# Two more k v products joined to other small products, the last gates in another order, and three moved steps in an attention and feed-forward kernel

## The chip, the cores and the metric

The kernel runs on one core of a Trainium2 chip. The time is the device time of one execution in microseconds (us); of several runs the median is given. The profile is of one further execution, whose own time is given beside it.

## The reference

```python
# q, k, v: (8, 8, 576, 64) = batch, head, sequence, head dimension
kv = np.einsum('bhsd,bhse->bhde', k, v)
out = np.einsum('bhsd,bhde->bhse', q, kv)
rms = np.sqrt(np.mean(out * out, axis=-1, keepdims=True) + 1e-06)
attn = out / rms * g_norm
# the bridge: heads side by side
x = attn.transpose(0, 2, 1, 3).reshape(4608, 512)
# the feed-forward part, d_ff = 1024
a = x @ w1
b = x @ w2
h = (a * b) @ w3
out = h @ w_out                        # (4608, 512)
```

Everything is float32. There is no softmax: attention is linear, so k v is a 64x64 matrix for each head.

## The kernel before

**What is worked on.** w3 and w_out are multiplied together once, early on (`fold_chunk`, L682, up to about 83 us), so that each token needs x, then `a * b` (the *gates*), then one product with the folded matrix (the *projection*). The 4608 tokens go in nine groups. Groups 0 to 7 hold 512 tokens of one batch each; the last 64 tokens of each of the eight batches, the *leftovers*, make up group 8. The loop `for n, T in enumerate(groups)` takes T in the order 0, 1, 2, 3, 4, 5, 6, 8, 7. While TensorE works on the gates of group T, the attention of batch T + 1 is strewn between its products.

**Strassen-Winograd products.** A gates stage multiplies 2x2 blocks with seven products in place of eight (`winograd`): sums of blocks s1 to s4 and t1 to t4 go in, and a11 b11, s1 t1, s2 t2, s4 b22, s3 t3, a12 b21, a22 t4 come out. The results are added up partly in the banks of PSUM (a product may be accumulated on top of an older one in the same bank) and partly by VectorE; c11, c12, c21, c22 are the four blocks of the result. Each product is four matmuls of 128x256 (L708), so a stage has 28. In the profile a matmul counts as two instructions, the weight load and the product: "x56" is one stage. ScalarE copies a bank that is still needed to SBUF (`keep`, L726: p1, p5, u2, u3), VectorE forms the c and multiplies its a half by its b half. Where `done` gets two summands it adds them on VectorE first; with one (c21) ScalarE copies one half (L854), and VectorE multiplies the other by it.

**Stages.** Of the four quarters of d_ff, p0 to p3, groups 0 and 1 do each in a gates stage of its own. Groups 2 to 8 (`IN_TWO`) do, in this order: gates p2; p0 and p1 together in a two-level Winograd product (`gates_of_two`, 98 matmuls of 128x128, L976, in two halves w = 0, 1 with seven products n each); gates p3, the *last gates*; and `project_twice` (L1223, again two-level, 98 matmuls). Between these stand `sum_ab` and `sum_ab_two`, which form the sums that the projection takes in, and `sum_inner`, which forms the inner sums of one of its seven products (numbers 0 to 6; `sum_inner(1, 2)` does two at once in instructions of twice the size). In the last gates VectorE's order is written by hand: `following` says what comes after which c. The inner sums of 1 and 2 are formed after c21, that is, after the last product.

**Attention pieces.** `steps(b)` lists what batch b does, in eight places fs[0] to fs[7]; one is run at each call of `between()` in group b - 1. In groups 2 to 6, places 0 and 1 lie in gates p2, 2 to 5 after products 2 and 5 of the two halves of `gates_of_two`, and 6 and 7 in the last gates. The pieces: `kv(g)`, k v of four heads, 36 small matmuls (L335), six copies to SBUF on ScalarE (L343, L345); `product(h)`, q times k v of four heads (L413) and the norm behind it (square, reduce, root, multiply); `product_left`, the same for the leftovers of two batches, for odd b only (L432). `kv(0)` of batch b + 1 is run in fs[6] while batch b is the current one, that is, in the last gates; `begin_kv` then issues the loads of `kv(1)`, and where g is 1 the loads of the next batch's k and v. These small products take their banks from `ps_at` (3 banks, the gates have `ps_mm`, 5 banks); the first bank of `product` comes from `ps_mm` if `of_mm` says so.

**Turns.** q and x must be transposed. Their pieces are `turn`, `begin` and `end`: copies on ScalarE, a DMA transpose, copies back. For b of 2 and over `turns_by_scalar` hangs each one on a *slot*: a name of a place such as ("p1", "u2"), run by `run_slot` right after the copy u2 of stage p1 has been issued. For b = 1 `steps` does it with `begin` and `end` behind a copy given by name. `end` of a q turn also issues the load of the next batch's q (`load_q_ahead`).

**Order and queues.** The order of TensorE, GpSimd and SyncE is that of the program. ScalarE and VectorE are ordered by a scheduler, with hints (`issue_after`), except VectorE in the last gates and the projection. SyncE's DMA queue issues in order: q, k, v, the streamed blocks of the weights (`load_w`), and those of the folded matrix (`load_b`, some of which go out on ScalarE's queue), and the stores.

Of the kernel before, what the change touches and what calls it, by code (L numbers as in the profile page):

```python
# [22 lines left out]
def kernel(  # L23
# [32 lines left out]
    nc = tc.nc  # L56
# [261 lines left out]
    def attention(b):  # L318
# [4 lines left out]
        def start():  # L323
            xT[b] = work.tile([P, 2, 2, NP // 2, N], FP32, name="xT")

        def kv(g):

            k_sb, v_sb = (loaded[name, b, g] for name in "kv")
            kv_ps = [bank(ps_at, "at")[:, 0:D] for _ in range(2)]
            for j in range(JS):  # L330
                cols = slice(j * D, (j + 1) * D)
                for r in range(2):
                    for e, ps in enumerate(kv_ps):
                        rows = slice(e * HP, (e + 1) * HP)
                        nc.tensor.matmul(  # L335
                            ps[r * D:(r + 1) * D, :],
                            lhsT=k_sb[rows, r, cols],
                            rhs=v_sb[rows, r, cols],
                            start=(j == 0),
                            stop=(j == JS - 1),  # L340
                        )
            for e, ps in enumerate(kv_ps):
                nc.scalar.copy(kv_b[:, 0, e, g, :], ps)  # L343
                for r in range(2):
                    copies["kv"] = nc.scalar.copy(  # L345
                        kv_b[(1 - r) * D:(2 - r) * D, 1, e, g, :], ps[r * D:(r + 1) * D, :]
                    )
# [51 lines left out]
        def product(h):  # L399

            of_mm = b and not (h and b > FIRST_OF_TWO)
            o_ps = [bank(*((ps_mm, "mm") if of_mm else (ps_at, "at"))), bank(ps_at, "at")]
            for m in range(4):
                r, e = 2 * h + m // 2, m % 2
                for i in range(2):
                    n = 2 * m + i
                    for t in range(2):
                        tokens = slice(t * L, (t + 1) * L)  # L410
                        for l in range(2):
                            rows = slice(l * D, (l + 1) * D)
                            nc.tensor.matmul(  # L413
                                o_ps[l][tokens, n * D:(n + 1) * D],
                                lhsT=qT[r][rows, e, i, tokens],
                                rhs=kv_b[rows, m // 2 ^ l, e, h, :],
                                start=True,
                                stop=True,
                            )
            xn = st[h] = work.tile([P, 2, 2, 4, D], FP32, name="xn", bufs=1)  # L420
            return norm(o_ps, [xn[:, :, l].rearrange("p i m d -> p m i d") for l in range(2)])

        def product_left():

            xn = st["left"] = work.tile([P, NP, 2, D], FP32, name="xn_left", bufs=1)

            o_ps = [bank(ps_at, "at") for _ in range(2)]
            for r in range(NP):
                for l in range(2):
                    for e in range(2):  # L430
                        rows = slice(e * D, (e + 1) * D)
                        nc.tensor.matmul(  # L432
                            o_ps[e][l * L:(l + 1) * L, r * D:(r + 1) * D],
                            lhsT=st["qT"][rows, r, l * L:(l + 1) * L],
                            rhs=kv_sb[(b - 1 + l) % 3][rows, r % 2 ^ e, e, r // 2, :],
                            start=True,
                            stop=True,
                        )
            o_ps = [t[:, 0:NP * D] for t in o_ps]
            all_of(norm(o_ps, [xn[:, :, e:e + 1, :] for e in range(2)]))  # L440

# [35 lines left out]
            elif b + 1 < B:  # L477
                load_q(b + 1, r + 2 - NP)

        def begin_kv(g):  # L480
            kv(g)
            if g == 0:
                load_four("kv", b, 1)
            elif b + 1 < B:
                load_four("kv", b + 1, 0)
# [38 lines left out]
    def turns_by_scalar(b):  # L524
# [14 lines left out]

        def end(name):  # L540
            all_of(turning[name])
            if name[0] == "q" and name[1] != "left":
                batch(name[1]).load_q_ahead(name[2])

        if b > FIRST_OF_TWO:
            q_begins, q_ends = ((0, 0), (0, 0)), ((0, 6), (1, 0))
# [20 lines left out]
        if b + 1 < B:  # L567
            n = batch(b + 1)
            for r in range(2):
                at(("p3", "u2"), begin, ("q", b + 1, r), n.q_by_dma, r)  # L570
                at(("proj", "u2"), end, ("q", b + 1, r))

    def steps(b):

# [26 lines left out]
        if b == 1:  # L601
# [8 lines left out]
                    all_of(t)  # L610

            ends[1].append((end_first,))
        fs[2 if b == 1 else 1] += [(a.begin_kv, 1), (a.finish, 0)]
        if b == 1:
            last = {}

            def begin(name, behind, f, *args):
                last[name] = f(*args)
                with tc.issue_after(copies[behind][-1].ins):
                    next(last[name])  # L620
                next(last[name])

            def end(name, behind):
                with tc.issue_after(copies[behind][-1].ins):
                    next(last[name], None)
                all_of(last[name])

            fs[2] += [(begin, f"q{r}", "u2", a.q_two_by_dma, r) for r in (2, 3)]
            fs[3].append((begin, "left", "u3", a.q_left_by_dma))
            fs[4].append((begin, "x", "u3", a.x_by_dma, 0, nc.scalar.copy))  # L630
            ends[4] += [(end, "q2", "p1"), (end, "q3", "p5")]
            ends[5] += [(end, "x", "u2"), (end, "left", "u3")]
        elif by_scalar:
            turns_by_scalar(b)
        else:
            turn(1, a.q_two_by_dma, 2, 3)
            turn(2, a.x_by_dma, 0)
            if odd:
                turn(1, a.q_left_by_dma)
        second = 5 if b == 1 else 4  # L640
        if more:
            fs[6 if in_two else second].append((batch(b + 1).begin_kv, 0))
        fs[second].append((a.finish, 1))
        if odd:
            fs[3 if in_two else second + 1].append((a.product_left,))
# [51 lines left out]

    def winograd(
        lhsT, rhs, chunks, done, between=lambda: None, keep_u3=True, after=lambda: None,
        places=(2, 1, 0),  # L700
    ):


        def product(a_name, b_name, to=None):
            ps = to if to is not None else bank(ps_mm, "mm").rearrange("p (u n) -> p u n", u=2)
            for u in range(2):
                for c in range(chunks):
                    nc.tensor.matmul(  # L708
                        ps[:, u, :],
                        lhsT=lhsT(a_name, u, c),  # L710
                        rhs=rhs(b_name, c),

                        start=(u == 0 and c == 0 and to is None),
                        stop=(c == chunks - 1),
                        skip_group_check=True,
                    )
            after()
            return ps

        def keep(name, ps):  # L720
            if name == "p1":
                t = pair_of_sums[:, 0].rearrange("p s c t -> p (s c) t")
            else:
                t = late_slots(places[("p5", "u2", "u3").index(name)])
# [2 lines left out]
            run_slot((stage[0], name), copies[name][-1])  # L727
            late[name] = t
            return t

        r1 = product("a11", "b11")
        p1 = keep("p1", r1)
# [111 lines left out]
    def gates(T, p, between, ready=lambda name: None):  # L844
# [4 lines left out]
        def multiply(name, one, two):  # L849
# [14 lines left out]
            lambda name, c: xb[T][name][:, c, :],  # L864
            NP // 2, done, between, T == 0 or p + 1 < NF,
            places=(2, 1, 0) if T not in IN_TWO else (0, 1, 2) if p + 1 == NF else (2, 0, 1),
        )


# [287 lines left out]

    inner = {}

    def sum_inner(*ns, between=lambda: None):  # L1160

        x_1 = ab[1].rearrange("p f j n -> p j f n")
        if ns == (1, 2):
# [2 lines left out]
            x = x_1  # L1166
        else:
            n, = ns
            x = {0: ab[0][:, :, 0], 3: ab_sums[2], 4: ab[0][:, :, 1], 6: x_1[:, 1]}[n].unsqueeze(1)
        a11, a12, a21, a22 = (  # L1170
            x[:, :, 2 * j:2 * j + 2, i * P:(i + 1) * P] for i in range(2) for j in range(2)
        )
# [2 lines left out]
        else:  # L1175
            s1, s2, s4 = (
                t.unsqueeze(1) for t in (
                    inner_sums[n % 4 // 3] if n < 6 else [pair_of_sums[:, 0, i] for i in range(3)]
                )
            )  # L1180
        nc.vector.tensor_add(s1, a21, a22)
        nc.vector.tensor_sub(s2, s1, a11)
        nc.vector.tensor_sub(s4, a12, s2)
        between()
        nc.vector.tensor_sub(a21, a11, a21)
        for i, n in enumerate(ns):
            inner[n] = [t[:, i] for t in (a11, a12, a22, s1, s2, s4, a21)]

    def project_twice(T, last, ahead, load_after):
        def store(half):  # L1190
# [99 lines left out]
        products(3, r2)  # L1290
        if not done[T]:
            load_b()
        if last:
            sum_inner(6)
            finish(p1, 0, 0)
# [140 lines left out]
    for n, T in enumerate(groups):  # L1436
# [44 lines left out]
        for p in range(NF):  # L1481
# [2 lines left out]
            stage[0] = f"p{p}" if T in IN_TWO or T == FIRST_OF_TWO - 1 else None  # L1484
            if T and p + 1 == NF:
                sum_1, sum_2, sum_4, sum_3 = sum_ab(p)
                following = {
                    "c12": [], "c22": [sum_1], "c11": [lambda: sum_inner(0, between=sum_2)],
                    "c21": [*of_two, lambda: sum_inner(1, 2), sum_3, sum_4],
                }  # L1490
# [100 lines left out]
```

## Time and profile before

| what | before |
|---|---|
| three runs | 746.58, 746.49, 746.93 us |
| median | 746.58 us |
| the profiled execution | 747.45 us |
| its span in the trace | 745.7 us |
| its granted TensorE clock | 1.0 |

The span is from the first to the last recorded instruction. By stretches of the span, busy microseconds of each engine and the share of the time in which the core's DMA engines are busy:

| stretch (us) | what runs | PE | VectorE | ScalarE | DMA |
|---|---|---|---|---|---|
| 0 to 83 | w3 times w_out, batch 0 | 79.41 | 68.11 | 60.55 | 0.93 |
| 131 to 217.4 | gates of group 1 and what lies ahead | 85.53 | 65.47 | 37.05 | 0.90 |
| 217.4 to 239.74 | projection of group 1 | 22.13 | 20.56 | 8.20 | 0.94 |
| 239.74 to 313.54 | group 2 | 73.80 | 63.80 | 40.63 | 0.85 |
| 313.54 to 386.52 | group 3 | 72.98 | 63.24 | 38.05 | 0.82 |
| 533.30 to 606.03 | group 6 | 72.73 | 63.67 | 35.48 | 0.65 |
| 606.03 to 673.97 | group 8 (leftovers) | 67.94 | 58.06 | 17.50 | 0.53 |

Groups 4 and 5 are like 2 and 3 (73.80 and 72.98 long). Where PE's time equals the length of the stretch, TensorE had no gap that the trace shows. An instruction's line is that of the function that issues it; the lines of helpers (L708, L726, L1025) are shared by all their callers, so a stage is told by its place in time or its tile.

### The profile page before, as it was taken

The page shows a single profiled execution, that of the slowest core. Times are in us where ns is not written, and L with a number is a line of the kernel's source. Part 1 is how long each engine was busy: PE and PEld are TensorE (multiplying, and loading weights), DVE is VectorE, ACT ScalarE, POOL GpSimd, SP SyncE. Part 2 cuts the span into 40 slices and gives each one's busy share as a digit, 9 for nine tenths or more (in the row PEclk, how much of TensorE's full clock was granted, in tenths as well). Part 3 has the DMA queues.
Part 4 walks back from the last instruction along what each step waited for, and adds up shares of the span by engine and source line. Part 5 has one row for each costly group of instructions (what it writes and reads, how often), then busy time and mean ns, then how long its engine had stood idle before and what let it go on. Part 6 is the DMA issues. An engine that isn't in the chain of part 4 may idle for free.

```text
span 745.7 us, 16769 instructions
## 1 busy us (share of the span) xinstructions
PE 737.3 (99%) x6843; PEld 658.5 (88%) x6843; DVE 632.7 (85%) x1212; ACT 371.2 (50%) x638; POOL 21.5 (3%) x29
## 2 busy tenths in 40 slices
PE   8999999999999999999999999999999999999998
PEld 5455788888899999999999999999999999999997
DVE  6987998967868699979996999799969987997797
ACT  6687878414552575256526752575267313212321
POOL 0000000131000000010000000000001000000000
PEclk9999999999999999999999999999999999999999
DMA  9996934598999689968987898579847672465454
GB/s 310 365 308 215 263 107 122 124 333 288 275 310 329 172 218 268 312 165 233 276 284 169 252 295 270 179 240 265 290 107 218 209 224 87 157 228 166 133 199 136
DMA packets 135456, 169.65 MB, mean 228 GB/s; under 512 B 78036, under 2 KB 110804, under 8 KB 135380
## 3 DMA queue, kind: packets, MB, share of 16 engines
q1 hardware_dynamic: 132928, 154.16, 68.9%
q10 hardware_dynamic: 2452, 14.42, 5.6%
q8 instruction: 54, 0.88, 0.5%
q14 instruction: 22, 0.18, 0.1%
HBM read 130.55 MB, written 20.71 MB: 203 GB/s over the span
## 4 chain that ended last, share of the span: by engine, by line
PE 94%; DMA 2%; DVE 1%; ACT 1%; issue 0%; SPq 0%; ACTq 0%; DVEq 0%
PE mm L708 38%; PE mm L1223 22%; PE mm L976 21%; PE mm L682 7%; PE at L335 2%; PE at L413 1%; DMA raw<-in_moe_w_out_dram 1%; PE at L669 1%; DMA w3o_sb<-w3o_l 1%; PE mm L413 1%; DMA raw<-in_moe_w_dram 0%; PE at L1266 0%; PE at L432 0%; ACT w_sb L133 0%; DVE c L859 0%; ACT qT L296 0%
## 5 line engine op out<-in xcount | busy, mean ns | idle before, releaser
L1025 ACT COPY slots<-mm 128x512 f32<-128x512 f32 x88 | 51.6, 586 | 131.4 <-PE mm L1223 73.4
L708 PE MATMUL mm<-xT,w_sb 128*128 128x256 f32 x480 | 110.2, 379 | 0.0
L708 PEld LDWEIGHTS mm<-xT,w_sb 128*128 128x128 f32 x480 | 90.4, 190 | 12.1 <-issue 0.5
L708 PE MATMUL mm<-xc,ws 128*128 128x256 f32 x352 | 79.8, 380 | 0.9 <-ACT inner_sums L726 0.9
L708 PEld LDWEIGHTS mm<-xc,ws 128*128 128x128 f32 x352 | 66.9, 190 | 10.2 <-ACT inner_sums L726 1.3
L726 ACT COPY slots<-mm 128x512 f32<-128x512 f32 x61 | 35.8, 587 | 70.9 <-PE mm L708 66.7
L682 PE MATMUL mm<-chunks,ab 128*128 128x512 f32 x128 | 60.7, 605 | 1.2 <-DVE chunks L172 1.2
L1029 DVE TENSOR_TENSOR slots<-mm,slots 128x512 f32<-128x512 f32 x66 | 45.3, 686 | 17.7 <-PE mm L976 17.3
L1026 ACT COPY slots<-mm 128x384 f32<-128x384 f32 x88 | 42.4, 482 | 24.9 <-PE mm L1223 22.3
L976 PE MATMUL mm<-ws,w3o_sb 128*128 128x128 f32 x350 | 54.0, 275 | 0.0
L1223 PE MATMUL mm<-w3o_sb,ab 128*128 128x128 f32 x368 | 48.7, 275 | 0.2 <-DMA w3o_sb<-w3o_l 0.2
L976 PEld LDWEIGHTS mm<-ws,w3o_sb 128*128 128x128 f32 x350 | 46.4, 192 | 0.0
L1223 PEld LDWEIGHTS mm<-w3o_sb,ab 128*128 128x128 f32 x368 | 45.4, 192 | 0.8 <-issue 0.4
L381 DVE TENSOR_REDUCE inv<-sq 128x8 f32<-128x512 f32 (+1 forms) x40 | 24.5, 628 | 25.3 <-ACT sq L380 25.0
L1223 PE MATMUL mm<-w3o_sb,raw 128*128 128x128 f32 x340 | 43.5, 275 | 0.0
L708 PE MATMUL mm<-xc,w_sb 128*128 128x256 f32 x176 | 42.4, 384 | 0.3 <-ACT slots L726 0.3
L682 PEld LDWEIGHTS mm<-chunks,ab 128*128 128x128 f32 x128 | 21.6, 190 | 22.9 <-issue 14.3
L1223 PEld LDWEIGHTS mm<-w3o_sb,raw 128*128 128x128 f32 x340 | 40.7, 192 | 0.0
L708 PE MATMUL mm<-xT,ws 128*128 128x256 f32 x160 | 38.5, 384 | 0.0
L708 PEld LDWEIGHTS mm<-xc,w_sb 128*128 128x128 f32 x176 | 32.8, 190 | 5.3 <-ACT slots L726 0.7
L1030 DVE TENSOR_TENSOR slots<-mm,slots 128x384 f32<-128x384 f32 x66 | 36.4, 551 | 0.9 <-PE mm L1223 0.9
L854 ACT COPY c<-mm 128x256 f32<-128x256 f32 x22 | 8.2, 371 | 54.1 <-PE mm L708 51.2
(230 smaller groups left out, 1634.2 us busy)
## 6 DMA issues: line engine op xcount, KB each, us to landing
w3o_sb<-w_l SPq DMA_DIRECT2D x21, 896.0 KB, 5.3
w3o_sb<-w3o_l SPq DMA_DIRECT2D x18, 896.0 KB, 4.7
raw<-in_moe_w_dram SPq DMA_DIRECT2D x31, 512.0 KB, 7.8
raw<-w3o_l SPq DMA_DIRECT2D x15, 896.0 KB, 4.8
w3o_sb<-w3o_l ACTq DMA_DIRECT2D x14, 896.0 KB, 4.7
k_sb<-in_k_dram SPq DMA_DIRECT2D x16, 576.0 KB, 4.9
v_sb<-in_v_dram SPq DMA_DIRECT2D x16, 576.0 KB, 6.1
q_sb<-in_q_dram SPq DMA_DIRECT2D x32, 256.0 KB, 4.5
```

The costliest lines, as they stand in the source:

```text
L335: nc.tensor.matmul(ps[r * D:(r + 1) * D, :], lhsT=k_sb[rows, r, cols], rhs=v_sb[rows, r, cols], start=(j == 0), stop=(j == JS - 1),)
L381: adds["norm"] = nc.vector.tensor_reduce(out=inv[:, i], in_=sq.rearrange("p (h d) -> p h d", d=D), axis=AX.X, op=ALU.add)
L413: nc.tensor.matmul(o_ps[l][tokens, n * D:(n + 1) * D], lhsT=qT[r][rows, e, i, tokens], rhs=kv_b[rows, m // 2 ^ l, e, h, :], start=True, st ...
L682: nc.tensor.matmul(sums_ps[half][m], lhsT=w3T[half, c][:, m, :], rhs=chunks[:, c, 1, :], start=(c == 0), stop=(c == KF - 1),)
L708: nc.tensor.matmul(ps[:, u, :], lhsT=lhsT(a_name, u, c), rhs=rhs(b_name, c),  start=(u == 0 and c == 0 and to is None), stop=(c == chunks ...
L726: copies.setdefault(name, []).append(nc.scalar.copy(t, ps))
L976: nc.tensor.matmul(ps[place // 4][:, place % 4, :], lhsT=x, rhs=y, start=new and place // 4 not in seen, stop=True, skip_group_check=True,)
L1025: nc.scalar.copy(z[:, 0:4], ps[0])
L1026: return nc.scalar.copy(z[:, 4:7], ps[1][:, 0:3])
L1029: nc.vector.tensor_add(z[:, 0:4], ps[0], z[:, 0:4])
L1030: nc.vector.tensor_add(z[:, 4:7], ps[1][:, 0:3], z[:, 4:7])
L1223: nc.tensor.matmul(ps[place // 4][:, place % 4, :], lhsT=x[:, c, :], rhs=y[:, c, :], start=new and place // 4 not in seen, stop=(c == 1), ...
```

## The change

- `kv` and `begin_kv` take `beside`, banks to put k v in: the last D columns of each. `kv(0)` of the next batch leaves the last gates of groups 2 to 5. For odd b over 2 `product_left` calls it with its own two banks, after its matmuls; for even b it goes in place `second` (4) ahead of `finish(1)`, which runs `product(1)`. For even b the first bank of that product comes from `ps_mm` now.
- The last gates of groups 2 to 8 go another way through `winograd` (`copy_first`). The order of the products becomes a11 b11, s1 t1, s2 t2, a12 b21, s3 t3, s4 b22, a22 t4. ScalarE copies a11 b11 from its bank into a second bank, r3, and a12 b21 is accumulated on top of it, so c11 comes out of one bank like c21 did. u3 is copied to the tile `inner_sums` (where p1 was kept). In groups 3 and 5 the first bank comes from `ps_at`.
- VectorE's order in these last gates: `following` has one sum each of inner 0, 1 and 2 in chosen places (`steps_of_inner` returns them one at a time), and 1 and 2 are no longer done as a pair.
- Group 1, gates: the remaining steps of the norm of batch 2's first q k v product (`begin_first`) go in the slot behind p1 of stage p1. Group 0: the turn of q3 begins one place later, behind u3. Projections: the load of q for the batch after (`load_q_ahead`) goes from the end of the q turn into the slot ("proj", "loads"), after `products(3)` and its `load_b`.

```diff
-        def kv(g):
+        def kv(g, beside=None):
...
-            kv_ps = [bank(ps_at, "at")[:, 0:D] for _ in range(2)]
+            kv_ps = [t[:, -D:] for t in beside or [bank(ps_at, "at") for _ in range(2)]]
...
-            of_mm = b and not (h and b > FIRST_OF_TWO)
+            of_mm = b and (h == 0 or b <= FIRST_OF_TWO or b % 2 == 0)
...
+            if FIRST_OF_TWO < b < B - 1:
+                batch(b + 1).begin_kv(0, o_ps)
             o_ps = [t[:, 0:NP * D] for t in o_ps]
...
         def end(name):
             all_of(turning[name])
-            if name[0] == "q" and name[1] != "left":
-                batch(name[1]).load_q_ahead(name[2])
+            if name[0] == "q" and name[1] == b:
+                a.load_q_ahead(name[2])
...
                 at(("proj", "u2"), end, ("q", b + 1, r))
+                at(("proj", "loads"), n.load_q_ahead, r)
...
-        fs[2 if b == 1 else 1] += [(a.begin_kv, 1), (a.finish, 0)]
+        def begin_first():
+            rest = a.product(0)
+            next(rest)
+            slots.setdefault(("p1", "p1"), []).insert(0, (all_of, rest))
+
+        fs[2 if b == 1 else 1] += [
+            (a.begin_kv, 1), (begin_first,) if by_scalar and not in_two else (a.finish, 0),
+        ]
...
-            fs[2] += [(begin, f"q{r}", "u2", a.q_two_by_dma, r) for r in (2, 3)]
+            fs[2].append((begin, "q2", "u2", a.q_two_by_dma, 2))
+            fs[3].append((begin, "q3", "u3", a.q_two_by_dma, 3))
...
         if more:
-            fs[6 if in_two else second].append((batch(b + 1).begin_kv, 0))
+            if not (in_two and odd):
+                fs[second].append((batch(b + 1).begin_kv, 0))
...
         def keep(name, ps):
-            if name == "p1":
+            if name == "p1" or copy_first and name == "u3":
...
+        if copy_first:
+            r1 = halves(first if first is not None else bank(ps_mm, "mm"))
+            r3 = halves(bank(ps_mm, "mm"))
+            product("a11", "b11", r1, new=True)
+            copies["p1"].append(nc.scalar.copy(r3, r1))
+            run_slot((stage[0], "p1"), copies["p1"][-1])
+            r2 = product("s1", "t1")
+            p5 = keep("p5", r2)
+            product("s2", "t2", r1)
+            u2 = keep("u2", r1)
+            between()
+            product("a12", "b21", r3)
+            done("c11", r3, None)
+            product("s3", "t3", r1)
+            done("c22", p5, keep("u3", r1))
+            product("s4", "b22", r2)
+            between()
+            done("c12", r2, u2)
+            product("a22", "t4", r1)
+            done("c21", r1, None)
+            return
...
+            copy_first=T in IN_TWO and p + 1 == NF,
+            first=bank(ps_at, "at") if T in IN_TWO and p + 1 == NF and T % 2 and T + 2 < B else None,
...
+        return [
+            lambda: nc.vector.tensor_add(s1, a21, a22),
+            lambda: nc.vector.tensor_sub(s2, s1, a11),
+            lambda: nc.vector.tensor_sub(s4, a12, s2),
+            lambda: nc.vector.tensor_sub(a21, a11, a21),
+        ]
...
+        for f, *args in slots.pop(("proj", "loads"), []):
+            f(*args)
...
+                zero, one, two = (steps_of_inner(n) for n in range(3)) if T in IN_TWO else [None] * 3
                 following = {
+                    "c11": zero[0:3], "c22": [],
+                    "c12": [sum_1, sum_3, sum_2, one[0], zero[3], one[1]],
+                    "c21": [
+                        one[2], one[3], *of_two, two[0], sum_4, two[1], two[2], two[3],
+                    ],
+                } if T in IN_TWO else {
                     "c12": [], "c22": [sum_1], "c11": [lambda: sum_inner(0, between=sum_2)],
                     "c21": [*of_two, lambda: sum_inner(1, 2), sum_3, sum_4],
                 }
```

More of the change, by code (lines that the diff above doesn't have):

```diff
@@ L478, in load_q_ahead, with begin_kv @@
                 load_q(b + 1, r + 2 - NP)
-        def begin_kv(g):
-            kv(g)
+        def begin_kv(g, beside=None):
+            kv(g, beside)
             if g == 0:
@@ L699, in winograd, with halves, product @@
         lhsT, rhs, chunks, done, between=lambda: None, keep_u3=True, after=lambda: None,
-        places=(2, 1, 0),
+        places=(2, 1, 0), copy_first=False, first=None,
     ):
-        def product(a_name, b_name, to=None):
-            ps = to if to is not None else bank(ps_mm, "mm").rearrange("p (u n) -> p u n", u=2)
+        def halves(ps):
+            return ps.rearrange("p (u n) -> p u n", u=2)
+        def product(a_name, b_name, to=None, new=False):
+            new = new or to is None
+            ps = halves(bank(ps_mm, "mm")) if to is None else to
             for u in range(2):
@@ L711, in product @@
                         rhs=rhs(b_name, c),
-                        start=(u == 0 and c == 0 and to is None),
+                        start=(u == 0 and c == 0 and new),
                         stop=(c == chunks - 1),
@@ L1158, with steps_of_inner @@
     inner = {}
-    def sum_inner(*ns, between=lambda: None):
+    def steps_of_inner(*ns):
         x_1 = ab[1].rearrange("p f j n -> p j f n")
@@ L1168, in sum_inner @@
             n, = ns
-            x = {0: ab[0][:, :, 0], 3: ab_sums[2], 4: ab[0][:, :, 1], 6: x_1[:, 1]}[n].unsqueeze(1)
+            x = {
+                0: ab[0][:, :, 0], 1: ab_sums[0], 2: ab_sums[1], 3: ab_sums[2], 4: ab[0][:, :, 1],
+                6: x_1[:, 1],
+            }[n].unsqueeze(1)
         a11, a12, a21, a22 = (
@@ L1177, in sum_inner @@
                 t.unsqueeze(1) for t in (
-                    inner_sums[n % 4 // 3] if n < 6 else [pair_of_sums[:, 0, i] for i in range(3)]
-                )
-            )
[L1181 to L1185, printed above, removed]
+                    [pair_of_sums[:, n % 2, i] for i in range(3)] if n in (1, 2, 6)
+                    else inner_sums[n % 4 // 3]
+                )
+            )
         for i, n in enumerate(ns):
             inner[n] = [t[:, i] for t in (a11, a12, a22, s1, s2, s4, a21)]
+        return [
[4 more added lines that the diff above has]
+        ]
+    def sum_inner(*ns, between=lambda: None):
+        *others, replace = steps_of_inner(*ns)
+        all_of(f() for f in others)
+        between()
+        replace()
     def project_twice(T, last, ahead, load_after):
```

## The prediction

> **What bounds the kernel now.** I read the page's first part, then who waited for whom, then the chain of waits, then the timelines of single stages.
>
> ```profile
> span 745.7 us, 16769 instructions
> ...
> PE 737.3 (99%) x6843; PEld 658.5 (88%) x6843; DVE 632.7 (85%) x1212; ACT 371.2 (50%) x638; POOL 21.5 (3%) x29
> ```
>
> TensorE is never free for long, and the chain of waits lies on it for 94% of the span, at a granted clock of 1.0. So a change can pay in two ways only: fewer microseconds of TensorE work, or fewer gaps in it. After 83 us the waits of PE are three:
>
> ```profile
> PE mm L708 <- ACT inner_sums L726: 0.9, 1, 0.9
> PE mm L708 <- ACT slots L726: 0.3, 1, 0.3
> PE mm L1223 <- DMA w3o_sb<-w3o_l: 0.2, 1, 0.2
> ```
>
> The chain (start, length, what) gives the price of each block, because a block of equal length that is interrupted or not can be compared:
>
> ```profile
> 313.54 10.36 PE mm L708 x48
> 323.90 1.21 PE at L335 x72
> ...
> 326.05 1.93 PE mm L708 x8
> 327.97 15.63 PE mm L976 x140
> 343.60 1.09 PE at L413 x64
> 344.69 6.45 PE mm L976 x56
> 351.14 5.18 PE mm L708 x24
> 356.32 1.21 PE at L335 x72
> 357.53 7.10 PE mm L708 x32
> ...
> 571.72 12.09 PE mm L708 x56
> 583.80 22.22 PE mm L1223 x196
> 606.03 12.09 PE mm L708 x56
> 618.12 21.88 PE mm L976 x196
> ```
>
> A gates stage alone is 12.09, 196 instructions of 128x128 alone are 21.88. From these: k v and q kv together cost 327.97 - 313.54 - 12.09 = 2.34; q kv alone costs 351.14 - 327.97 - 21.88 = 1.29; k v alone costs 364.63 - 351.14 - 12.09 = 1.40. Apart they are 2.69, so a place where the two follow each other saves 0.35. In the same way leftovers alone (group 2, 254.17 to 278.16, less 21.88 and 1.29) cost 0.82. Groups 2 to 5 hold nothing beyond these blocks: 73.80 = 67.94 + 2.34 + 0.82 + 1.29 + 1.40 within 0.01. The gaps are elsewhere: 0.34 in group 6's projection (22.22 for 21.88), 0.45 in group 1's (217.41 to 239.74), 1.13 in group 1's gates (173.61 to 196.08 is 22.47; 88 L708 instructions and 2.34 make 21.34), and about 0.4 at 121.4 in group 0.
>
> **The joined k v.** In groups 2 to 5 the 36 matmuls leave the last gates: for odd b (groups 2, 4) they go behind the leftovers, for even b (3, 5) ahead of the second q kv product. Four joins at 0.35 are 1.40. Those with q kv repeat a pair that the trace shows. One with the leftovers isn't shown; it saves between 0 and 0.35, and I take 0.35, as both are 64x64 blocks like the shown pair. So 1.40, at least 0.70.
>
> What moves with them: six ScalarE copies (L343, L345) and two loads of 576 KB on SP. At 174.87 the six take 1.32. In groups 3 and 5 they end about when the q kv product does, and the two squares behind them start 0.3 late; ScalarE has 0.48 of waiting next (345.82), so nothing is passed on. In groups 2 and 4 they stand ahead of the leftovers' squares and of the copy of the next p1 (L1025, 267.68 to 268.27), which TensorE needs at 268.89: cover 0.62. k v gives the queue 1.05 more on PE; 1.32 of copies and a square of 0.28 then push that copy to about 269.86, against 269.94 for PE. I take 0.1 lost over both groups, from 0 to 0.4.
>
> Here the Trainium skill speaks against the join: "TensorEngine Tiling (Array Packing)", Performance Considerations, PSUM Bottleneck, says that tiling speeds up TensorE but not the emptying of PSUM, which may become the bottleneck. Were the emptying the bound, 1.32 - 0.62 = 0.70 would be lost in each of two groups, 1.40 in all, and the sum would be 1.2 instead of 2.6. The row's 4.3 us of ScalarE idle in the same group's last gates (before 291.69) says the queue is late in places only, so I stay with the rows.
>
> The two loads move before SP's q loads in groups 2 and 4, behind them in 3 and 5. DMA is busy 0.91 of 264 to 278 and 0.95 of the last gates, so 1.15 MB (some 5 us at 216 GB/s) displace what follows by about 5. q at 267.92 took 4.4 and is copied at 284.17; the three w3o loads from 274.84 on are needed from 291.7 on. Both have more than 5 left. The k v loaded for the leftovers' place is issued at 251.3 and 251.84 and lands in 5.7 and 6.7, by 258.5, needed at 263.9.
>
> **The last gates (groups 2 to 8).** TensorE's 28 matmuls stay 28. ScalarE gets r3<-r1, u3 and one c21 copy, and loses p1: +0.58 + 0.37 per group, on an engine that is half idle. VectorE loses the 0.69 add of c11, and sums of inner 1 and 2 become eight of 0.42 for four of 0.69: +0.6; net 0. What counts is when each must be ready, counted from the start of the last gates (s), with VectorE free at 8.1 as before (L1071 ends 8.17 after 278.16):
> - r3 copy: starts 1.77, PE overwrites r1 at 3.45. Bank to bank isn't shown; the nearest rows are 0.37 (128x256) and 1.18 (L158, 128x1024). Cover 1.68 holds both. I take 0.58, the row of equal size.
> - c11: PE done 6.91; ScalarE has two qT copies to 7.9, c21 to 8.3, the multiply to 8.7, three sums to 9.9; the projection (12.09) needs them from 13.4 on.
> - c22 waits for u3 (9.3), is done by 11.0; c12 by 12.2; then sum_1, sum_3, sum_2, one, zero's last: 13.97, needed 14.77. Cover 0.8, the thinnest. c21's multiply ends 14.6.
> - inner 1: s4 and s3 by 15.4, needed 17.45 and 17.9. Before, s3 came at 18.78 after its start and was needed at 19.3 with k v's 1.4 in between; in group 6, without k v, that was the 0.34 of 22.22.
> So nothing is lost, and the 0.34 goes. If VectorE were 1 later, every group would lose 0.2.
>
> **Group 1's gates.** ScalarE's queue (start, length):
>
> ```profile
> 177.71 0.37 ACT L854 COPY c<-mm 128x256 f32<-128x256 f32 x1 [0.43 <-PE mm L708]
> 181.17 0.31 ACT L385 ACTIVATE inv<-inv,eps_col 128x16 f32<-128x16 f32 x1 [3.09 <-DVE inv L381]
> 181.38 0.56 ACT L726 COPY inner_sums<-mm 128x512 f32<-128x512 f32 x1
> 181.85 1.04 ACT L296 COPY qT<-q_sb 128x1024 uint16<-128x1024 uint16 x1
> 182.80 0.58 ACT L726 COPY slots<-mm 128x512 f32<-128x512 f32 x1
> ```
>
> The root waits 3.09 for VectorE, and p1's copy stands behind it. After, p1 goes at 179.2 and PE goes on at 180.97. But VectorE's reduces still end at 181.13 (its backlog comes from a DMA at 173.76), the root and one qT copy still come before p5, so p5 ends at 182.91 and PE wants it at 182.7: a gap of 0.25 and the restart of 0.11 (2.00 for 1.89). The two xn products move behind seven sums to 185.83, xT's two copies behind them to 187.8, u3 to 188.38, PE wants it at 188.24: 0.15 and 0.11 again. So 1.13 becomes 0.65, gain 0.48; from 0.2 to 1.13.
>
> **Group 1's projection.** The load for its last product is issued at 229.95, behind two q loads (228.40), and takes 6.3; the median of the tile's loads is 4.7. With the q loads behind it lands at 234.7, before 236.2. Gain 0.45, from 0. In other groups SP's order is unchanged.
>
> **Group 0.** The second qT copy (1.05) and its transpose move behind u3. But the root before u3 waits for reduces that end at 120.97, and it started at 121.00. Gain 0.03, from 0 to 0.4; the qT copies then end 1 us later, with 2.8 of ScalarE idle at 132.55.
>
> **Sum.** 1.40 - 0.10 + 0.34 + 0.48 + 0.45 + 0.03 = 2.6. The profiled execution has a span of 745.7 and took 747.45; so 743.1 and 744.85. The runs' median is 746.58, 0.87 below the profiled one; the same 2.6 off gives 744.0.
>
> **Rivals.**
> - All gaps go: 1.40 + 0.34 + 1.13 + 0.45 + 0.40 = 3.72, so 742.9. For: each edit sits at a gap. Against: VectorE's backlog at 181.13 and 120.97 isn't touched. 0.10.
> - Only the joins pay; the gaps reappear where p5, u3 or another queue is next: 745.2. For: VectorE is 85% busy and 21.09 of 21.9 in group 2's projection. Against: sums that come 2 earlier. 0.14.
> - The change doesn't do what it says: the joins save nothing, because k v's 1.40 is work wherever it stands; 2.6 - 1.4 leaves 745.4. Against: the pair at 323.90. 0.05.
> - Slower: in groups 2 and 4 q lands late behind k v. ScalarE's qT copies then hold c11's c21 copy and VectorE behind it. I expect landing near 280.5 and use at 285.2, and 0.8 of cover in the projection. It decides from 5.5 later on; to undo 2.6 and add 1.5 takes 2.05 more in each, so 7.5 later: 748.1. For: DMA 0.91 and 0.95 busy. Against: the same bytes leave the last gates. 0.07.
> The forecast has 0.64.
>
> **Numbers.** The lower bounds together (0.70 - 0.40 + 0.2 + 0.03) leave 0.5, so 746.0; the upper are 742.9. The range is 742.8 to 746.0, with the slower rival and a little of the others outside. 0.2% is 1.5 us, about what a measurement of this kernel can tell from no change; faster than 745.1 are the forecast and the first rival: 0.74. Within: 0.19, slower 0.07.
>
> **What would show it.** k v adjoining L432 or L413 and last gates of 12.09 whole in groups 2 to 5 (right); a projection of 21.88 in groups 1 and 6; group 1's inner_sums wait gone, small waits for slots in its place. Wrong: PE waits for ab or inner_sums in the projections, for slots L1025 in groups 2 and 4, or ScalarE waiting for q_sb.

## The result and the profile after

| | before | after |
|---|---|---|
| median of 21 runs each | 746.72 us | 745.11 us |
| ratio, 95% interval | | 0.9979, 0.9973 to 0.9985 |
| profiled execution | 747.45 us | 745.00 us |
| its span | 745.7 us | 743.1 us |

The kernel became 1.6 us faster, where 2.6 was forecast; 745.11 lies in the range of 742.8 to 746.0. The two spans differ by the 2.6 us that the sum gave. The step from 2.6 to 1.6 is mostly the choice of execution: the profiled one of before was 0.73 above the median of its runs, that of after 0.11 below. And within the 2.6 several terms were wrong and made up for each other.

The first part of the page of after, then its waits of PE after 83 us:

```profile
span 743.1 us, 16816 instructions
...
PE 736.6 (99%) x6843; PEld 659.5 (89%) x6843; DVE 629.4 (85%) x1233; ACT 378.7 (51%) x652; POOL 21.8 (3%) x29
```

```profile
PE mm L724 <- ACT slots L742: 0.3, 1, 0.3
```

PE carries out the same 6843 instructions with the same 6843 weight loads. (The 28 matmuls of a gates stage stand as 56 MATMULs under PE and as 56 loads under PEld. So a float32 matmul of this program is two MATMULs, each with its own load; the section on the kernel before took the second of the two for the load.) Two of the three waits of before are gone; the one that is left is that of group 0. The view of the waits names none of the new ones, which are too short for it; the chain of after shows them in the lengths of its pieces (start, length, what):

```profile
216.22 21.88 PE mm L1274 x196
...
261.91 0.62 PE at L432 x32
262.53 1.05 PE at L335 x72
263.58 6.61 PE mm L1016 x56
...
277.74 12.09 PE mm L724 x56
289.82 22.02 PE mm L1274 x196
...
341.90 1.21 PE at L335 x72
344.04 6.45 PE mm L1016 x56
...
362.58 21.95 PE mm L1274 x196
...
436.26 22.09 PE mm L1274 x196
...
509.09 21.96 PE mm L1274 x196
...
581.56 21.93 PE mm L1274 x196
```

Group 1's projection is 21.88, without a gap. At 261.91 k v follows the leftovers and costs 1.05, at 341.90 it stands ahead of q k v and with that takes 2.14, where q k v alone took 1.09: again 1.05, instead of 1.40 by itself. The last gates are 12.09 whole. But 6.61 stands for 6.45, and the projections of groups 2 to 5 are 22.02, 21.95, 22.09 and 21.96, where they were 21.88. So of the signs that the prediction named, the joined k v, the whole last gates and the gone wait for `inner_sums` are there, and so are two that it named as wrong: PE waits for `ab` in the projections and for the slots of L1025 (here L1065) in groups 2 and 4. Both are shown in lines below.

The next table is made from the starts of the matmuls in each trace: the length of a stage is from its first matmul to that of the next, in us. From group 2 on, every stage that isn't listed is alike within 0.02 in all of them. The kernels of the last three columns come with the experiments; "last gates alone" is the second of its two runs.

| stage | before | after | joins alone | last gates alone | both |
|---|---|---|---|---|---|
| two-level gates, groups 2 / 4 | 23.99 / 23.99 | 25.21 / 25.21 | 25.21 / 25.21 | 23.99 / 23.99 | 25.21 / 25.22 |
| the same, groups 3 / 5 | 23.17 / 23.17 | 24.22 / 24.22 | 24.22 / 24.22 | 23.17 / 23.17 | 24.22 / 24.22 |
| last gates, 2 / 3 | 13.50 / 13.50 | 12.09 / 12.09 | 12.28 / 12.22 | 13.50 / 13.50 | 12.09 / 12.09 |
| last gates, 4 / 5 | 13.50 / 13.50 | 12.09 / 12.09 | 12.37 / 12.21 | 13.50 / 13.50 | 12.09 / 12.09 |
| projection, 2 / 3 | 21.88 / 21.88 | 22.01 / 21.95 | 22.24 / 22.24 | 21.88 / 21.88 | 22.01 / 21.96 |
| projection, 4 / 5 | 21.88 / 21.88 | 22.09 / 21.96 | 22.24 / 22.24 | 22.02 / 21.88 | 22.08 / 21.96 |
| projection, 6 | 22.22 | 21.93 | 22.23 | 21.88 | 21.88 |
| sum of groups 2 to 6 | 366.29 | 365.40 | 367.34 | 366.08 | 365.35 |

From group 2 on, then, the change gives 0.89. Most of the rest of the 2.6 is in group 1: 0.45 in the projection and 1.13 in the gates.

### The profile page after: what moved, and what is told of

Its sections match the earlier page's. It is cut to its first block, busy times and chain, and to the rows that moved or that the text cites. A ratio compares the mean times of both kernels' runs of the same rounds, so it can differ in the third digit from the quotient of the medians.

```text
span 743.1 us, 16816 instructions
## 1 busy us (share of the span) xinstructions
PE 736.6 (99%) x6843; PEld 659.5 (89%) x6843; DVE 629.4 (85%) x1233; ACT 378.7 (51%) x652; POOL 21.8 (3%) x29
## 4 chain that ended last, share of the span: by engine, by line
PE 96%; DVE 1%; ACT 1%; DMA 1%; issue 0%; SPq 0%; ACTq 0%
PE mm L724 37%; PE mm L1274 23%; PE mm L1016 21%; PE mm L694 7%; PE at L335 2%; PE at L724 2%; PE at L413 1%; PE mm L413 1%; PE at L681 1%; DMA raw<-in_moe_w_out_dram 1%; PE at L1317 0%; DVE ab L162 0%; PE at L432 0%; ACT w_sb L133 0%; DVE chunks L169 0%
## 5 line engine op out<-in xcount | busy, mean ns | idle before, releaser
L1065 ACT COPY slots<-mm 128x512 f32<-128x512 f32 x88 | 51.7, 587 | 125.7 <-PE mm L1274 83.1
L724 PE MATMUL mm<-xT,w_sb 128*128 128x256 f32 x448 | 102.9, 379 | 0.0
L724 PEld LDWEIGHTS mm<-xT,w_sb 128*128 128x128 f32 x448 | 84.4, 190 | 11.5 <-issue 0.5
L724 PE MATMUL mm<-xc,ws 128*128 128x256 f32 x336 | 76.1, 379 | 0.0
L724 PEld LDWEIGHTS mm<-xc,ws 128*128 128x128 f32 x336 | 63.8, 190 | 8.7
L724 PE MATMUL mm<-xc,w_sb 128*128 128x256 f32 x160 | 38.6, 384 | 0.3 <-ACT slots L742 0.3
L308 ACT COPY xT<-xn 128x1024 uint16<-128x1024 uint16 x28 | 32.5, 1168 | 3.3 <-DMA xn<-xT 3.3
L724 PEld LDWEIGHTS mm<-xc,w_sb 128*128 128x128 f32 x160 | 29.7, 190 | 4.9 <-ACT slots L742 0.7
```

What stands on the lines that cost most here:

```text
L308: copy(words(dst), src)
L724: nc.tensor.matmul(ps[:, u, :], lhsT=lhsT(a_name, u, c), rhs=rhs(b_name, c),  start=(u == 0 and c == 0 and new), stop=(c == chunks - 1), s ...
L1065: nc.scalar.copy(z[:, 0:4], ps[0])
```

## The experiments

**The kernel before, once more.**

> The kernel before, unchanged, profiled once more. The profile of before came from an execution of 747.45 us, 0.73 above the median of 21 runs. Theory 'lucky gap': part of the two gaps of group 1 (1.13 us in its gates behind VectorE's wait for a DMA at 173.76, 0.45 in its projection behind a load) is that execution's own, and this one shows less of them: the two together 0.5 to 1.0 and a span near 745.0. Rival 'fixed gap': both gaps stand again, 1.13 and 0.45 within 0.15, span 745.7; then the missing 0.8 us between the two profiles' 2.6 and the medians' 1.6 is elsewhere.

It took 747.92 us with a span of 746.1. The gap in group 1's gates is 0.23 here, not 1.13; the one in its projection is 2.17, not 0.45. So neither rival as written: the two gaps change from one execution to the next, and they don't shrink together. From group 2 on every stage is the same within 0.02.

**The joined k v alone.** Against the kernel before (`kv` and `begin_kv` take `beside` as in the change):

```diff
...
-            of_mm = b and not (h and b > FIRST_OF_TWO)
+            of_mm = b and (h == 0 or b <= FIRST_OF_TWO or b % 2 == 0)
...
+            if FIRST_OF_TWO < b < B - 1:
+                batch(b + 1).begin_kv(0, o_ps)
...
-            fs[6 if in_two else second].append((batch(b + 1).begin_kv, 0))
+            if not (in_two and odd):
+                fs[second].append((batch(b + 1).begin_kv, 0))
```

> The kernel before with the joined k v alone. Theory 'a pair': the joins save 4 x 0.35 on TensorE and lose 2 x 0.17 to the copy of p1 (groups 2 and 4), but with k v gone from the last gates every projection of groups 2 to 5 shows the 0.34 that only group 6 showed (22.22 for 21.88): 1.40 - 0.34 - 1.36 = -0.3, so 0.3 us slower than before, within what can be told. Rival 'the terms add': the joins pay 1.40 - 0.34 = 1.06 by themselves, and projections of groups 2 to 5 stay 21.88.

Ratio 1.0014, 1.0006 to 1.0023: slower, by 1.05 us. The chain of this kernel in group 2, from the last gates on:

```profile
278.82 12.28 PE mm L711 x56
291.10 22.24 PE mm L1226 x196
```

The projection's 0.35 is as "a pair" had it. In addition the last gates lose 0.12 to 0.28 each, which it had not: sum 1.05 by the stages of groups 2 to 6, 367.34 for 366.29, the same as the ratio says. What holds the last gates there is open. In the projection PE waits in the second product, for the inner sums of 1 and 2: VectorE makes them from 294.19 to 296.93, and PE comes to them from 295.40 on (first and last of the sums, then PE's twelve MATMULs, which take 1.70 for 1.50):

```profile
294.19 0.69 DVE L1184 TENSOR_TENSOR inner_sums<-raw 128x512 f32<-128x512 f32 x1
...
296.25 0.68 DVE L1188 TENSOR_TENSOR raw<-raw 128x512 f32<-128x512 f32 x1
```

```profile
295.40 1.70 PE L1226 MATMUL mm<-raw,inner_sums 128*128 128x128 f32 x12
```

That is the wait that only group 6 showed before, since the others had k v in the last gates to cover it.

**The last gates alone, twice.** With k v left in the last gates, the first of these kernels adds up other values for c11 in groups 3 and 5 than the reference has: it copies a11 b11 into another bank of PSUM than the changed kernel does, one whose last quarter, by the second expectation below, no product had filled. No trace shows that. The second takes the first bank of the last gates always from `ps_mm` and computes what the kernel before computes; it differs from the first in one line, and what is said of this part rests on it.

```diff
-            first=bank(ps_at, "at") if T in IN_TWO and p + 1 == NF and T % 2 and T + 2 < B else None,
+            first=None,
```

> The kernel before with the new order of the last gates alone; k v stays in them in groups 2 to 5. Theory 'a pair': group 6 gains 0.3, groups 2 to 5 have 1.4 us of k v as cover and neither gain nor lose: 0.3 us faster, projections 21.88 to 21.95 in all groups. Rival 'the terms add': the stall of the seventh sum of inner 0, 0.06 to 0.21 in each projection of groups 2 to 5, is there with k v too, 0.3 - 0.5 = 0.2 us slower.

> The kernel before with the new last gates alone, as in the first such run, but the first bank of the last gates always from the gates' own pool (in that run groups 3 and 5 copied a11 b11 into another bank than the changed kernel does, one whose last quarter a product had not filled, and so added up other values for c11). Theory 'a pair': projections 21.88 in all groups, group 6 gains 0.34, groups 2 to 5 stay 73.80 and 72.98; 0.3 us faster, which this measurement can't tell from nothing. Rival: with r3 in another bank PE waits for it, and the last gates of groups 3 and 5 are longer than 13.50.

Ratios 1.0003 (0.9994 to 1.0011) and 1.0001 (0.9992 to 1.0010). By the stages both gain 0.34 in group 6; the first changes nothing else, and in the second group 4's projection showed 0.14 more, once. With k v in the last gates the sums have 1.4 more time, and nothing is gained or lost, as "a pair" says. 0.3 is too little for the ratios to show.

**Both together, without the three moves.**

> The kernel before with the joined k v and the new last gates together, without the three moved steps. Theory 'a pair': each alone showed no gain, but together the last gates are 12.09 and the projections 21.93 to 22.09, so groups 2 to 6 give 0.06 + 0.29 - 0.03 + 0.28 + 0.30 = 0.9 us: ratio 0.9988, with group 1's projection still at 0.4 to 2.2 of gap. Rival 'each for itself': the sum of the two single runs, 1.1 slower and 0.0 to 0.3 faster, so 0.8 to 1.1 us slower than before.

Ratio 0.9988, 0.9979 to 0.9996, so 0.9 us faster; stages 365.35 for 366.29. One part alone costs 1.05, the other gives nothing that the times can tell, together they give 0.9. "Each for itself" is out.

**The moves, and the moved loads among them.** The first run is the kernel before with the three moves alone. The second is the changed kernel with the loads of q put back:

```diff
-            if name[0] == "q" and name[1] == b:
-                a.load_q_ahead(name[2])
+            if name[0] == "q" and name[1] != "left":
+                batch(name[1]).load_q_ahead(name[2])
...
-                at(("proj", "loads"), n.load_q_ahead, r)
```

> The kernel before with the three moved steps alone (the norm in group 1, the turn of q3 in group 0, the loads of q behind the loads of the folded matrix). Theory 'lucky gap': the profile shows no gap in group 1's gates and projection, but the median falls by 0.7 to 1.0 us only, since a usual execution of before had less than 1.58 of gaps. Rival 'fixed gap': 1.5 to 1.7 us faster.

> The changed kernel with the loads of q back ahead of the load of the folded matrix in the projections. Theory 'the queue': in group 1's projection 0.5 MB stand ahead of the last load on SP's queue, and the gap of 0.4 to 2.2 us of the runs without the move comes back: 0.4 to 1.3 us slower than the changed kernel, ratio to before 0.9985 to 0.9996. Rival 'the norm': what the moves gain comes from the norm in group 1's gates; then this run stays within 0.3 us of the changed kernel (0.9979), projection 21.88.

The moves alone: ratio 0.9981, 0.9972 to 0.9989, 1.4 us faster, between the two rivals. Its profiled execution, 747.32 us, was near the slowest of its twelve (745.23 to 747.56), with a group 1 projection of 23.55; the load of the streamed weights behind the q loads took 6.8 there where it takes 5.2 in after, and PE had several short gaps. The changed kernel without the moved loads: 0.9988, 0.9979 to 0.9997, and the gap is back. By the times alone this can't be told from the changed kernel, as the intervals overlap; the traces tell it. The chain of this kernel at group 1's projection:

```profile
216.64 12.52 PE mm L1273 x112
...
229.18 7.66 DMA w3o_sb<-w3o_l
...
236.97 3.36 PE mm L1273 x28
```

The load is issued at 229.18, behind two q loads (227.63), and takes 7.66. With the q loads behind it, the same load took 4.83 and 4.91 in the two profiles of the changed kernel, though it is issued no earlier in its stage. So "the queue" holds. In all, seven profiled executions without the moved loads had gaps there of 0.45, 2.17, 0.43, 1.70, 1.83, 1.81 and 1.33; of seven with them, six had none and one 1.67 (the moves alone, where this load took 6.83).

**The one late sum.** In the changed kernel, group 2: VectorE, then PE (start, length, line, out<-in).

```profile
291.22 0.42 DVE L805 TENSOR_TENSOR raw<-raw,ab 128x256 f32<-128x256 f32 x1
291.56 0.42 DVE L1228 TENSOR_TENSOR inner_sums<-raw 128x256 f32<-128x256 f32 x1
291.89 0.42 DVE L1231 TENSOR_TENSOR ab<-ab 128x256 f32<-128x256 f32 x1
```

```profile
291.00 1.50 PE L1274 MATMUL mm<-w3o_sb,raw 128*128 128x128 f32 x12
292.37 0.71 PE L1274 MATMUL mm<-w3o_sb,ab 128*128 128x128 f32 x4
```

The first L1231 is the last of the four sums of inner 0, which overwrites a21 (the expectations call it the seventh). It ends at 292.31, and PE goes on 0.06 later, at 292.37. Without a wait it would have been there at 292.34, 24 MATMULs after 289.66. Twelve usually take 1.34; here the next start 1.37 later, and the four take 0.71, not 0.61, as PE has to start anew: 0.13 in all. In group 4 it is 0.21 in all. Nothing between c11 and this sum needs to stand ahead of it:

```diff
-                    "c11": zero[0:3], "c22": [],
-                    "c12": [sum_1, sum_3, sum_2, one[0], zero[3], one[1]],
+                    "c11": zero, "c22": [],
+                    "c12": [sum_1, sum_3, sum_2, one[0], one[1]],
```

> The changed kernel with the seventh sum of inner 0 (in place of a21) directly behind the three others, after c11, not behind the sums after c12. Theory 'one late sum': it is what product 0 of the projection waits for in groups 2 to 6 (0.14, 0.06, 0.21, 0.08, 0.05); all projections become 21.88 and the time 0.5 us less than the changed kernel's: ratio to before about 0.997. Rival 'VectorE is full': c22, c12 and the sums of product 1 come 0.34 later and PE waits for those; projections stay 21.93 to 22.1.

> The changed kernel again, beside the others on one chip. All stages from group 2 on as in its first profile within 0.05 (projections 22.01, 21.95, 22.09, 21.96, 21.93), group 1's gates without a gap, its projection 21.88 or with a gap where the loads come slowly; ratio to before 0.997 to 0.998. Rival 'luck': group 1's projection shows a gap as often as without the moved loads.

> The changed kernel with the one early sum, again. 0.5 us less than the changed kernel on the same chip, all projections 21.88. Rival: the difference between the two medians is within 0.2, as other gaps take its place.

The chain of the first of these, groups 2 and 4:

```profile
290.08 21.88 PE mm L1274 x196
...
436.33 21.88 PE mm L1274 x196
```

All projections of groups 2 to 8 are 21.88, in both runs, so it gives 0.5 by the stages. On one chip the changed kernel took 745.18 (ratio to before 0.9974, 0.9961 to 0.9986) and this one 744.62 (0.9958, 0.9946 to 0.9970): 0.56 less, where 0.5 was expected. The two intervals overlap, so that it beats the changed kernel too rests on the stages. It is the one to keep. In the changed kernel's second run the stages from group 2 on were as in the first, within 0.02, and group 1's projection again had no gap; with one gap in seven executions against seven in seven, "luck" is out.

**The late copy of p1.** ScalarE and PE of the changed kernel in group 2, where 6.61 stands for 6.45:

```profile
267.73 0.58 ACT L1065 COPY slots<-mm 128x512 f32<-128x512 f32 x1
```

```profile
268.08 0.39 PE L1016 MATMUL mm<-sq,w_sb 128*128 128x128 f32 x2
268.37 0.71 PE L1016 MATMUL mm<-xc,w3o_sb 128*128 128x128 f32 x4
```

The copy ends at 268.31, behind six k v copies, two squares and the root. PE goes on at 268.37, again 0.06 after that end, where two matmuls after 268.08 would be 268.30, and loses 0.1 to start anew. To take this away, k v went to the second q k v product in groups 2 and 4 too, on top of the early sum:

```diff
-            of_mm = b and (h == 0 or b <= FIRST_OF_TWO or b % 2 == 0)
+            of_mm = b and (h == 0 or b < B - 1)
...
-            if FIRST_OF_TWO < b < B - 1:
-                batch(b + 1).begin_kv(0, o_ps)
...
-            if not (in_two and odd):
-                fs[second].append((batch(b + 1).begin_kv, 0))
+            fs[second].append((batch(b + 1).begin_kv, 0))
...
-            first=bank(ps_at, "at") if T in IN_TWO and p + 1 == NF and T % 2 and T + 2 < B else None,
+            first=bank(ps_at, "at") if T in IN_TWO and p + 1 == NF and T + 2 < B else None,
```

> As the run before, and k v joined to the second q k v product in groups 2 and 4 too, not to the leftovers (first bank of the last gates from the other pool in groups 2 to 5, that of the product from the gates' pool). Theory 'one late copy': the 0.17 that the two-level stage of groups 2 and 4 loses at the copy of p1 behind six k v copies goes, 25.04 for 25.21; 0.34 us less than the run before, 0.8 less than the changed kernel, ratio about 0.9967. Rival 'a copy is late somewhere': the six copies hold the copies of the next stage's banks instead, and the stage stays at 25.2.

> k v joined to the second q k v product in all of groups 2 to 5, again. If the gap of 0.7 us in the middle of group 4's q k v product (without a releaser) belongs to the program, it stands again at the same instruction and the time is 0.2 to 0.5 above the run beside it; if it was that execution's own, group 4 is 73.44 like group 2 and the time 0.34 below the run beside it.

Group 2's two-level stage is 25.04 in both, as forecast: 0.17 gone. Group 4's is 25.89 and 25.86: in its q k v product one matmul starts 0.7 after the one ahead of it, both times shortly before the product's end. The chain of the second run:

```profile
417.41 0.05 PE mm L413
417.46 0.50 issue
417.96 0.27 PE at L413
```

"issue" is time in which nothing that the profile shows held PE. It came in both executions, so it belongs to this program. The time was 744.77 beside 744.47 for the early sum alone and, on another chip, 745.42 beside 744.62; by the stages of groups 2 to 6 it is 0.5 slower both times. What makes the gap was not tried. In both runs one 16 KB packet of the queue that carries instructions starts 2.2 to 2.3 us before the gap's end; in the changed kernel such a packet starts 5.4 us ahead of that product. So a late fetch of instructions in a dense row of small matmuls is a guess, not shown.

## Why the prediction was right or wrong

- **The joins, 1.40.** Size right: 0.35 each, the untested one with the leftovers too. The rows show where it is. 0.19 is the change from large matmuls to small ones and back: in before, group 2, PE pauses 0.09 ahead of k v (283.27, where 16 regular steps from 279.73 give 283.18), and the first gates matmuls behind it take 1.99 for 1.89. The other 0.16 is that small products in a row start closer: leftovers and k v take 1.67 in after (261.84 to 263.51) and 0.62 + 1.21 apart in before (263.48 to 264.10, 283.27 to 284.48). As a term by itself it was wrong: alone the joins cost 1.05. They pay because the new last gates come with them, which the sum never said; it had the cause in sight ("with k v's 1.4 in between; in group 6, without k v, that was the 0.34 of 22.22") and did not apply it to the groups that lose k v.
- **The copy of p1, 0.1 lost over both groups (0 to 0.4).** Mis-sized: 0.17 in each, 0.34 together. The cover was 0.08 by the prediction's own numbers (269.86 against 269.94); the copy came 0.09 later than planned, PE needs 0.06 from its end, and the stop costs another 0.1 to start again. The Trainium skill ("TensorEngine Tiling (Array Packing)", Performance Considerations, PSUM Bottleneck) says that the copying out of PSUM may become the bottleneck. That pointed at the right place, but the 1.40 that the prediction worked out for that case is four times what was lost.
- **The last gates, nothing lost.** Wrong: 0.49 over groups 2 to 5. The step that failed is "zero's last: 13.97, needed 14.77. Cover 0.8, the thinnest". In after, group 2, counted from the first matmul at 277.57, that sum ends at 14.74, and PE needs 0.06 more.

```profile
283.96 2.00 ACT L296 COPY qT<-q_sb 128x1024 uint16<-128x1024 uint16 x2
285.85 0.38 ACT L892 COPY c<-mm 128x256 f32<-128x256 f32 x1
```

```profile
286.27 0.42 DVE L894 TENSOR_TENSOR ab<-c,mm 128x256 f32<-128x256 f32 x1 [0.16 <-ACT c L892]
286.72 0.43 DVE L1228 TENSOR_TENSOR raw<-ab 128x256 f32<-128x256 f32 x1
287.18 0.42 DVE L1229 TENSOR_TENSOR raw<-raw,ab 128x256 f32<-128x256 f32 x1
287.64 0.43 DVE L1230 TENSOR_TENSOR raw<-ab,raw 128x256 f32<-128x256 f32 x1
```

  Of the 0.77, 0.42 was there when c11's multiply ended (9.12 for 8.7), because ScalarE's qT copies and the copy for c11 ended at 8.39 and 8.66, not at 7.9 and 8.3. Two zero points may have a part in it: VectorE's 8.17 is counted from 278.16, where the chain has the stage begin, and the need of 14.77 fits the first matmul, 278.00, which makes the cover 0.16 too large. The three sums of zero, which wait for each other, start 0.46 apart, not 0.34 as free ones do, and took 1.38 for 1.2. The rest, 0.16 to 0.17, came behind c12, where one more sum starts 0.46 after the one before it. The spacing was in the trace of before (291.15, 291.61, 292.07). The text gave the case of a late VectorE its price, 0.2 a group, and left it out of the sum.
- **Group 6's 0.34 goes.** Right: 0.29, and all of it with the early sum.
- **Group 1's gates, 0.48.** The span lost 1.13 here, but by chance: the gap hung on VectorE's wait for a DMA until 173.76, which was that execution's.

```profile
173.76 0.42 DVE L1124 TENSOR_TENSOR raw<-raw 128x256 f32<-128x256 f32 x1 [5.11 <-DMA out_dram<-raw]
```

```profile
172.50 0.43 DVE L1164 TENSOR_TENSOR raw<-raw 128x256 f32<-128x256 f32 x1 [4.03 <-ACT slots L742]
```

  The first line is before, the second after. The step "VectorE's reduces still end at 181.13" failed: they ended at 179.87, in after and in the second run of before alike. In five other executions without the moved norm the gap was 0.23 once, and none in joins alone, both runs of the last gates alone, and both together. So no run shows a gain of the moved norm beyond that 0.23.
- **Group 1's projection, 0.45.** Mechanism right, size low: five of the seven gaps were 1.3 to 2.2, so the moved loads are the largest gain of the change in most of these executions. The first runs of before, at 746.72 against 747.41 to 747.63 in the later ones, would fit a small gap like that of their profile; another chip could do it too, and neither is shown.
- **Group 0, 0.03.** Nothing is seen there: the wait of 0.3 stands in both pages.
- **The rivals.** q late behind k v did not happen: the qT copies in group 2's last gates start at 283.96 without a wait. That the joins save nothing is refuted by the 1.05 for 1.40. "Only the joins pay" is the reverse of what was found. Of "all gaps go", the two of group 1 and most of group 6's went in after, but new ones came in groups 2 to 5 and group 0's stayed.

By stages the span's 2.6 is 1.40 - 0.34 - 0.49 + 0.29 = 0.86 in groups 2 to 6 (0.89 measured), and 0.45 + 1.13 in group 1; 0.07 lies ahead of 83 us. That the forecast hit the span to a tenth is luck: what the last gates lost (0.49) and the copy of p1 lost too much (0.24) was made up by a gap of group 1's gates that was of one execution.

## What to carry to other kernels

Small work in front of a stage covers waits that no view shows; before taking it away, look at the one place that already lacks it (here group 6) and charge its gap to every other. A gap behind a DMA that stands in one profile is one draw: profile the same kernel two or three times before a gain is worked out from it. When sums hang on each other, plan them by the dependent spacing, and put what the next stage asks for first ahead of what it asks for later.

## What the hardware showed that was not expected

- A 128x256 float32 sum on VectorE that needs the one before it starts 0.46 us after that one, a free one 0.34 (286.72 and 287.18; 291.22 and 291.56 in after).
- A stop of PE costs more than its wait: after the two pauses shown above the next matmuls of 128x128 lost another 0.1 (0.71 for 0.61), so a sum that held PE up for 0.03 cost 0.13. In both, PE went on 0.06 after the end of what it waited for.
- Copying 128x512 float32 from one PSUM bank to another took ScalarE 0.57 us in the last gates of after, to SBUF 0.59 on the mean.
- In a row of small matmuls of one program, PE started one 0.7 us after the other with no wait in the profile, at nearly the same place in two executions. The cause is open.
